# Token mixing placed between attention units, one PSUM pool for the whole program, and early conversion of four weight blocks

## The chip, the core and the metric

The kernel runs as one program on one NeuronCore of a Trainium2 chip. The metric is the time of one execution on the device in microseconds (us), measured from outside; three runs of the kernel before took 513.26, 514.47 and 515.23 us, median 514.47. Engines are named as in the profile: PE (TensorE matmuls; PEld is its weight load), DVE (VectorE), ACT (ScalarE), POOL (GpSimd) and SP (SyncE, which here issues the DMAs).

## What is computed

Two batches of 768 tokens pass through attention with 8 heads of 64 columns (a band of `n_local` = 96 keys behind each query, and `n_global` = 8 global keys, with a bias linear in distance), then through two mixing blocks. The calls chain as attention, `_moe_ref`, `_moe2_ref`; cut to what matters here:

```python
scores = scale * np.matmul(q, k.transpose(0, 1, 3, 2)) + bias      # kept in the band only
a = np.exp(scores - max);  a = a / (sum(a) + 1e-9);  x = a @ v      # x: (2, 768, 512)

xt = x.transpose(0, 2, 1)                       # _moe_ref: token mixing, then channel mixing
h  = np.maximum(xt @ w_tok1, 0.0) @ w_tok2      # 768 -> 256 -> 768 over tokens
u  = x + h.transpose(0, 2, 1)
x  = u + np.maximum(u @ w_ch1, 0.0) @ w_ch2     # 512 -> 1536 -> 512 over channels

theta = x @ w_theta                             # _moe2_ref
y = w_tok_r @ (x*cos(theta)) + w_tok_i @ (x*sin(theta))
out = (x + y) + np.maximum((x + y) @ w_ch, 0.0)
```

The weights arrive as 64-bit floats.

## The kernel before

Matrices of the mixing blocks are kept as two fp32r parts, a high and a low one, and each product is three matmuls (`mm3`: high by high, high by low, low by high).

**Jobs.** Each piece of a weight, 512 or 384 double words per partition, is loaded as raw words and converted on the chip by a "job" of four phases: `job_scale` (two ACT passes, lines 120 and 121), `job_join` (two DVE passes, lines 126 and 129, and one on POOL, line 130), `job_high` (ACT, line 138), `job_low` (DVE, line 141). One call of `tick` moves every running job by a phase, may start the next, and asks SP for further loads (two ahead, three raw buffers).

**Attention** (`attention_band`) goes over 24 units: batch, pair of heads, and two query blocks of 128; three units make up a pair of heads. In step u the code emits the scores of unit u (PE, line 383), per block and head the maximum with the bias (DVE, line 395) and the exponential (ACT, line 405); then, one by one in turn, the transposes of unit u-1 (PE, line 426, copied from PSUM by ACT, line 433) and the products with the values of unit u-2 (PE, line 350); then the division by the sum (`finish_rows`, DVE, lines 334 to 343), the split of x into its two parts (`x_split`, POOL, lines 323 and 326) and the tick. A job is started in the first unit of each pair of heads from the second pair on, seven in all: the weights of token mixing. The order on every engine is the order of this code. Scores use 4 PSUM banks, transposes 2, values 2.

**Mixing** (`moe`, after the attention, with new PSUM pools: 6 banks `acc`, 2 banks `wps`). The first product of token mixing (`token_mix`, "mm1": 18 matmuls for each of 2 batches and 2 blocks of 128 hidden tokens) runs for batch 0, block 0 in the last two steps of the attention, and for the other three blocks after it. `token_mix2` then runs the second product ("mm2") in 12 rows of 6 matmuls; DVE adds each row to x (line 803), and three rows later PE transposes it (line 621), ACT takes its high part (line 588) and DVE its low part (line 594). Every second row has a tick. `channel_mix` follows (`up`: matmuls "gp"; `down`: matmuls "h"), with the ticks for 24 channel jobs and for the weights of the last block, and then `PhaseB`.

**The start.** Whether the band form may be used depends on `n_global` and `n_local`: every engine loads these into registers (line 670), computes the condition and branches (line 678). The bias of the band (`band_bias`) is built from the same numbers, which DMA brings into the tile `nvi`: some dozen short DVE operations, and then one scaled copy for each of the 8 heads on POOL (line 273).

Of the kernel before, what the change touches and what calls it, by code (L numbers as in the profile page):

```python
# [24 lines left out]
P = 128  # L25
# [9 lines left out]
NG = 32  # L35
# [11 lines left out]
WARM = 12  # L47
# [13 lines left out]
def r(ap):  # L61
    return ap.bitcast(F32R)


class Build:
# [84 lines left out]
    def prefetch(self):  # L150
        while self.jobs and len(self.loaded) < self.AHEAD:
            job = self.jobs.pop(0)
            self.job_load(job)
            self.loaded.append(job)
# [7 lines left out]
    def tick(self, start=True):  # L162

        phases = (self.job_scale, self.job_join, self.job_high, self.job_low)
        for job in self.running:
            job["phase"] += 1
            phases[job["phase"]](job)
# [3 lines left out]
        self.prefetch()  # L171
        if start and self.loaded and self.loaded[0]["gate"] <= self.gate:
            job = self.loaded.pop(0)
            job["phase"] = 0
            phases[0](job)
            self.running.append(job)

# [10 lines left out]
    def constants(self, pool):  # L188
        nc = self.nc
        self.ident = pool.tile([P, P], F32, name="ident")  # L190
        make_identity(nc, self.ident)

        nvi = pool.tile([P, 4], I32, name="nvi")
        nc.sync.dma_start(out=nvi, in_=self.dram["nv"].broadcast_to([P, 4]))
        nvf = pool.tile([P, 4], F32, name="nvf")
        nc.vector.tensor_copy(out=nvf, in_=nvi)
# [11 lines left out]
        self.halfpi = pool.tile([P, 1], F32, name="halfpi")  # L208
        nc.vector.memset(self.halfpi, math.pi / 2)
        one = pool.tile([P, 1], F32, name="one")  # L210
        nc.scalar.activation(out=one, in_=self.halfpi, func=AF.Exp)

    def iota(self, pool, n, base, step, mult, name):
# [4 lines left out]
        return tf  # L218

    def band_bias(self, pool):  # L220
# [6 lines left out]
        ng, nl = self.nval[:, 0:1], self.nval[:, 1:2]  # L227
# [3 lines left out]
        with self.tc.tile_pool(name="bb", bufs=1) as tp:  # L231

            def ramp(n, base, mult, name):

                ti = tp.tile([P, n], I32, name=name + "_i")
                nc.gpsimd.iota(ti, pattern=[[1, n]], base=base, channel_multiplier=mult)
                tf = tp.tile([P, n], F32, name=name)
                nc.scalar.copy(out=tf, in_=ti)
                return tf

            def near(out, t, dist, tag):
# [7 lines left out]
            d_own = ramp(P, 0, -1, "own")  # L249
            d_prev = ramp(PREV, -PREV, -1, "prev")  # L250
            gcol = ramp(NG, 0, 0, "gcol")
            past = tp.tile([P, P], F32, name="past")
            nc.gpsimd.affine_select(
                out=past, in_=d_own, pattern=[[-1, P]], compare_op=ALU.is_ge, fill=-BIG,
                base=0, channel_multiplier=1,
            )
            nnl = tp.tile([P, 1], F32, name="nnl")
            nc.vector.tensor_scalar(out=nnl, in0=nl, scalar1=-1.0, scalar2=None, op0=ALU.mult)
            g = tp.tile([P, NG], F32, name="far_g")
            nc.vector.tensor_scalar(  # L260
                out=g, in0=gcol, scalar1=ng, scalar2=-BIG, op0=ALU.is_ge, op1=ALU.mult
            )
            nc.vector.tensor_scalar(out=seen, in0=g, scalar1=nl, scalar2=None, op0=ALU.subtract)
            near(own, past, d_own, "own")
            nc.vector.tensor_tensor(
                out=base0[:, 0:NG], in0=own[:, 0:NG], in1=seen, op=ALU.max
            )
            nc.vector.tensor_copy(out=base0[:, NG:P], in_=own[:, NG:P])
            near(before, d_prev, d_prev, "prev")
        self.base = []  # L270
        for h in range(H):
            t = pool.tile([P, 3 * P], F32, name="base%d" % h)
            nc.gpsimd.tensor_scalar(
                out=t, in0=base, scalar1=slope(h) / SCALE, scalar2=None, op0=ALU.mult
            )
# [4 lines left out]
    def warm_up(self, pool, n):  # L280

        ps = pool.tile([P, 512], F32, name="warm%d" % self.uid(), tag="o")
# [12 lines left out]

    def load_v(self, pool, t, b, hp, band=True):


        nc = self.nc
        n = "_%d_%d" % (b, hp)  # L300

# [840 lines left out]
```

## Time and profile before

| | |
|---|---|
| median of three runs | 514.47 us |
| profiled execution: time from outside / span of the trace | 513.04 / 511.0 us |
| start to the first maximum of unit 0 | 0 to 8.43 us |
| attention, 24 units | to 95.1 us |
| rest of mm1, three blocks | 96.44 to 109.07 us |
| mm2 and transposes, 12 rows | 109.07 to 132.10 us |
| channel mixing and PhaseB, to the last matmul | 132.10 to 507.9 us |

A row of a list of instructions begins with its start and its length in us, then engine, line of the kernel, operation, output<-input. The length of a matmul includes the filling and emptying of the array, so that neighbours overlap: the pace of PE is read from one start to the next. What stands in brackets is the idle time before the instruction and what ended it.

### The profile page before, as it was taken

What the parts mean: (1) busy time and instruction counts of PE and PEld (TensorE: products, weight loads), DVE (VectorE), ACT (ScalarE), POOL (GpSimd) and SP (SyncE); (2) the same over time, 40 slices, a digit from 0 to 9 for tenths busy, and PEclk for the clock granted to TensorE, in tenths of its full rate; (3) what the DMA queues carried; (4) which work ended last, traced back from release to release, by engine and by line L of the source; (5) the groups of instructions that cost most, each with busy time, mean ns of one, the idle gap of its engine ahead of it and who ended that gap; (6) DMA issues with size and microseconds to landing.
All of it is one profiled execution on the core that took longest, in us unless ns stands there. A gap on an engine that the chain in (4) does not pass through costs nothing.

```text
span 511.0 us, 7727 instructions
## 1 busy us (share of the span) xinstructions
PE 498.8 (98%) x2910; PEld 421.6 (83%) x2910; DVE 303.0 (59%) x669; ACT 238.9 (47%) x463; POOL 166.6 (33%) x175
## 2 busy tenths in 40 slices
PE   7999999999899999999999999999999999999997
PEld 3887888787788888888888888888888888888886
DVE  4677776269985754114655465387888885452352
ACT  4888878347665551102454453444555434132010
POOL 6654454133333331000333141234555543222000
PEclk9999999999999999999999999999999999999999
DMA  7867645144444440001433111321220000000012
GB/s 230 271 204 196 176 128 182 47 124 137 141 145 145 129 130 0 1 0 42 123 125 124 42 41 50 115 84 48 86 73 1 1 1 1 21 22 21 22 62 104
DMA packets 29724, 45.93 MB, mean 90 GB/s; under 512 B 1904, under 2 KB 20592, under 8 KB 29680
## 3 DMA queue, kind: packets, MB, share of 16 engines
q1 hardware_dynamic: 29680, 45.36, 29.1%
q8 instruction: 25, 0.41, 0.3%
q14 instruction: 19, 0.16, 0.1%
HBM read 42.21 MB, written 3.15 MB: 89 GB/s over the span
## 4 chain that ended last, share of the span: by engine, by line
PE 88%; DVE 7%; ACT 2%; DMA 1%; issue 1%; DVEq 0%; ACTq 0%
PE gp L77 20%; PE y L77 20%; PE h L77 19%; PE th L77 7%; PE v L77 7%; PE o L350 6%; PE t L426 4%; PE s L383 3%; PE mm L77 3%; ACT e L405 1%; DVE x L803 1%; DVE cvs L126 1%; DVE xl L594 1%; DVE cvt L129 1%; DVE wc L141 1%
## 5 line engine op out<-in xcount | busy, mean ns | idle before, releaser
L130 POOL TENSOR_TENSOR cvt<-cvt,cvs 128x512 int32<-128x512 int32 (+1 forms) x57 | 75.8, 1330 | 211.5 <-DVE cvt L129 197.0
L77 PE MATMUL h<-wc,g 128*128 128x512 f32 x432 | 102.2, 390 | 0.0
L77 PE MATMUL gp<-xh,wc 128*128 128x512 f32 (+1 forms) x384 | 99.0, 339 | 1.6 <-DVE xl L594 1.6
L77 PEld LDWEIGHTS h<-wc,g 128*128 128x128 f32 x432 | 79.6, 188 | 15.5
L590 DVE SCALAR_TENSOR_TENSOR g<-gp,g 128x512 fp32r<-128x512 f32 (+1 forms) x48 | 26.7, 557 | 91.2 <-ACT g L588 91.2
L77 PEld LDWEIGHTS gp<-xh,wc 128*128 128x128 f32 x384 | 67.1, 188 | 11.1 <-DVE xl L594 1.8
L77 PE MATMUL gp<-xl,wc 128*128 128x512 f32 (+1 forms) x192 | 64.9, 338 | 0.0
L588 ACT ACTIVATE g<-gp 128x512 fp32r<-128x512 f32 (+1 forms) x48 | 23.5, 489 | 78.8 <-PE gp L77 78.8
L77 PE MATMUL y<-wri,z 128*128 128x256 f32 (+1 forms) x288 | 52.9, 338 | 0.0
L77 PE MATMUL y<-wri,s 128*128 128x256 f32 (+1 forms) x288 | 52.8, 338 | 0.0
L426 PE MATMUL t<-ident,e 128*128 128x128 f32 x176 | 48.0, 285 | 3.5 <-ACT at L433 3.5
L77 PEld LDWEIGHTS y<-wri,s 128*128 128x128 f32 x288 | 44.9, 188 | 6.8
L77 PEld LDWEIGHTS y<-wri,z 128*128 128x128 f32 x288 | 44.8, 188 | 6.7
L405 ACT ACTIVATE e<-e,mn 128x256 f32<-128x256 f32 (+1 forms) x96 | 39.3, 481 | 17.5 <-DVE mn L395 17.5
L126 DVE SCALAR_TENSOR_TENSOR cvs<-cvt,cvs 128x512 int32<-128x512 int32 (+1 forms) x57 | 43.9, 770 | 0.0
L426 PEld LDWEIGHTS t<-ident,e 128*128 128x128 f32 x176 | 31.7, 185 | 11.7 <-ACT at L433 11.3
L77 PEld LDWEIGHTS gp<-xl,wc 128*128 128x128 f32 x192 | 36.1, 188 | 5.2
L120 ACT ACTIVATE cvt<-raw 128x512 f32<-128x512 f32 (+1 forms) x57 | 37.6, 659 | 2.2 <-issue 2.2
L121 ACT ACTIVATE cvs<-raw 128x512 int32<-128x512 uint16 (+1 forms) x57 | 37.6, 660 | 0.0
L395 DVE CUSTOM_DVE_ANT_0 e<-s,base 128x256 f32<-128x256 f32 (+1 forms) x96 | 32.8, 395 | 5.3 <-PE s L383 2.7
L932 ACT ACTIVATE w<-w 128x512 f32<-128x512 f32 x12 | 7.6, 632 | 57.3 <-DVE w L929 57.3
L350 PE MATMUL o<-v,at 128*128 128x65 f32 x192 | 32.3, 252 | 0.0
(140 smaller groups left out, 799.1 us busy)
## 6 DMA issues: line engine op xcount, KB each, us to landing
raw<-w_ch SPq DMA_DIRECT2D x28, 512.0 KB, 3.5
raw<-w_tok SPq DMA_DIRECT2D x21, 512.0 KB, 3.5
k<-k SPq DMA_DIRECT2D x8, 480.0 KB, 4.0
q<-q SPq DMA_DIRECT2D x8, 384.0 KB, 3.2
v<-v SPq DMA_DIRECT2D x8, 384.0 KB, 4.2
out<-o SPq DMA_DIRECT2D x11, 256.0 KB, 2.0
raw<-w_theta SPq DMA_DIRECT2D x4, 512.0 KB, 3.5
a<-v SPq DMA_DIRECT2D x8, 240.0 KB, 4.7
```

Source lines behind the costliest of these rows:

```text
L77: self.nc.tensor.matmul(out, lhsT=a, rhs=b, start=first and i == 0, stop=last and i == n - 1)
L120: nc.scalar.activation(out=f(t), in_=f(top), func=AF.Copy, scale=2.0**-111)
L121: nc.scalar.activation(out=s, in_=nxt, func=AF.Copy, scale=2.0**-13)
L126: nc.vector.scalar_tensor_tensor(out=s, in0=t, scalar=-(1 << 31), in1=s, op0=ALU.bitwise_and, op1=ALU.bitwise_or)
L130: nc.gpsimd.tensor_tensor(out=t, in0=t, in1=s, op=ALU.add)
L350: self.nc.tensor.matmul(po[:, j * OW : j * OW + D + 1], lhsT=at, rhs=v[:, j * (D + 1) : (j + 1) * (D + 1)], start=first, stop=last,)
L383: nc.tensor.matmul(ps[j][:, ii, c0:], lhsT=t["q"][pj, i * P : (i + 1) * P], rhs=kf[pj, i * KW - P + c0 : i * KW + P], start=True, stop=True,)
L395: nc.vector.tensor_tensor_reduce(out=e, in0=ps[j][:, ii, c0:], in1=self.base[2 * hp + j][min(i, 1)], op0=ALU.add, op1=ALU.min, scale=-SCAL ...
L405: nc.scalar.activation(out=e, in_=e, func=AF.Exp, bias=mn[:, ii, j : j + 1], scale=-1.0,)
L426: nc.tensor.transpose(pt[:, ii, c, :], e[j][:, ii, c * P : (c + 1) * P], self.ident)
L588: nc.scalar.activation(out=hi, in_=ps, func=AF.Relu if relu else AF.Copy)
L590: nc.vector.scalar_tensor_tensor(out=lo, in0=ps, scalar=0.0, in1=f(hi), op0=ALU.max, op1=ALU.subtract)
```

## The change

- All PSUM tiles come from one pool for the whole program, with tags s (4 banks), o (1), m (1) and t (2); what was `acc` goes around s, s, s, s, o, m.
- mm1 of batch 0 stands in units 14 to 19 of the attention (two parts of 3 matmuls behind each unit), its mm2 rows in steps 20 to 25 and the first four of its transposes in steps 22 to 25; mm1 of batch 1 and the last two transposes stand at the end of the attention. `token_mix2` has the 6 rows of batch 1 alone.
- From unit 12 on the values of all units use the one bank o (before that o and m in turn).
- Eleven jobs are started in the attention, at units given by a table: the seven of token mixing and four channel pieces, which get buffers of their own.
- Within a unit the DVE passes of jobs stand behind the maxima, and in the units that start a job behind one of the copies as well; two of the four exponentials stand behind the first copy of the transposes, and the ACT passes of jobs ahead of the second. In units that start a job, up to unit 19, DVE makes the first copy.
- The start: register loads and branch stand ahead of the bias; the bias takes its numbers without the 64-bit arithmetic, two of its steps are on POOL; ACT makes the scaled copies of heads 0 and 1; q and k of the first pair of heads come in two pieces each, and v after the branch; 10 warm-up matmuls instead of 12.

```diff
+class Banks:
+    BUFS = dict(s=4, o=1, m=1, t=2)
+        self.round = itertools.cycle("ssssom")
+    def tile(self, shape, dtype, name, tag):
+        if tag == "acc":
+            tag = next(self.round)
+        return self.pool.tile(shape, dtype, name=name, tag=tag, bufs=self.BUFS[tag])
...
+    def split_tick(self, start):
+        on_act = [job for job in self.running if job["phase"] % 2]
+        on_dve = [job for job in self.running if not job["phase"] % 2]
+        def act():
+            self.advance(on_act)
+            self.begin(start)
+        return functools.partial(self.advance, on_dve), act
...
         for h in range(H):
             t = pool.tile([P, 3 * P], F32, name="base%d" % h)
-            nc.gpsimd.tensor_scalar(
-                out=t, in0=base, scalar1=slope(h) / SCALE, scalar2=None, op0=ALU.mult
-            )
+            if h < 2:
+                nc.scalar.activation(out=t, in_=base, func=AF.Copy, scale=slope(h) / SCALE)
+            else:
+                nc.gpsimd.tensor_scalar(
...
+                        if j == 1:
+                            between()
+                        if j == 0 and dve:
+                            nc.vector.tensor_copy(out=af, in_=pf)
+                        else:
+                            nc.scalar.copy(out=af, in_=pf)
...
-                po = ps_o.tile([P, 2, 2 * OW], F32, name="o" + n, tag="o")
+                tag = "m" if u < half and u % 2 else "o"
+                po = ps_.tile([P, 2, 2 * OW], F32, name="o" + n, tag=tag)
...
+            for n in range(2 * NS):
+                tb, s = divmod(n, NS)
+                fill[half + 2 + n // 2].append(mix1(0, tb, s, "m"))
+            for s in range(NS):
+                fill[N - 4 + s].append(mix2(s))
+            for s in range(4):
+                fill[N - 2 + s].append(columns(s))
+            for tb in range(NT):
+                for s in range(NS - 2):
+                    fill[N + 1].append(mix1(1, tb, s, "s"))
...
+                start = u in self.STARTS
+                on_dve, on_act = self.split_tick(start)
...
-                    scores(u)
+                    exps = scores(u)
-                else:
-                    self.token_mix(ps_s, h1, 0, 0, tag="s", part=u - N)
+                if not start:
+                    on_dve()
+                for step in exps[:2]:
+                    step()
+                def between(late=exps[2:]):
+                    for step in late:
+                        step()
+                    if start:
+                        on_dve()
+                    on_act()
...
-                if oi:
-                    self.tick(start=u < N and ip == 0)
+                for step in fill.pop(u, ()):
+                    step()
...
+            for tb in range(NT):
+                for s in range(NS - 2, NS):
+                    mix1(1, tb, s, "s")()
+            for s in range(4, NS):
+                columns(s)()
...
+    EARLY = 4
+    STARTS = (5, 8, 11, 13, 14, 16, 17, 18, 20, 21, 22)
...
-        for b, tb in ((0, 1), (1, 0), (1, 1)):
-            self.tick()
-            self.token_mix(acc, h1, b, tb)
-        self.tick()
-        pend = self.token_mix2(acc, wps, h1)
+        pend = self.token_mix2(h1)
```

Three places where the order of instructions differs. First, DVE at the start of the program, before; `nv` are the two numbers as registers, `base` the bias, `s_0` the scores and `mn` the maxima of unit 0.

```order
L265 TENSOR_TENSOR base<-base 128x32
L247 TENSOR_TENSOR base<-farprev,prev 128x96
L670 TENSOR_LOAD nv_ptr
L670 TENSOR_LOAD nv
L678 ISA
L678 REGISTER_ALU
L678 ISA
L678 REGISTER_ALU x2
L678 COMPARE_AND_BRANCH
L395 ISA e_0_337,mn_336<-s_0_339,base_181 128x128
```

The same engine after the change, from its first memset on.

```order
L851 MEMSET zero 128x256
L225 MEMSET halfpi 128x1
L856 TENSOR_LOAD nv_ptr
L856 TENSOR_LOAD nv
L861 ISA
L861 REGISTER_ALU
L861 ISA
L861 REGISTER_ALU x2
L861 COMPARE_AND_BRANCH
L287 CAST nvf<-nvi 128x4
L294 TENSOR_SCALAR nnl<-nvf 128x1
L299 TENSOR_SCALAR farown<-ramp_130,nnl 128x128
```

The loads and the branch have moved from between the bias and the first maximum to ahead of the bias.

Second, DVE in a unit in which a job is joined, before (unit 8; `cvs` and `cvt` are the job's tiles, `o` the products with the values).

```order
L343 TENSOR_TENSOR x_83<-o_668,rc_689 128x2x128
L126 SCALAR_TENSOR_TENSOR cvs_648<-cvt_647,cvs_648 128x512
L129 TENSOR_SCALAR cvt_647<-cvt_647 128x512
L395 ISA e_8_712,mn_711<-s_8_714,base_189 128x256
L395 ISA mn_711 128x1
```

And after (unit 6).

```order
L447 ISA e_6_595,mn_593<-s_6_597,base_310 128x256
L447 ISA mn_593 128x1
L142 SCALAR_TENSOR_TENSOR cvs_585<-cvt_584,cvs_585 128x512
L145 TENSOR_SCALAR cvt_584<-cvt_584 128x512
L387 TENSOR_SCALAR rc_636<-o_611 128x4
L391 RECIPROCAL rc_636<-rc_636 128x4
```

The job's two passes stood ahead of the unit's four maxima and now stand behind them, ahead of `finish_rows`.

Third, PE between the values of a unit and the scores of unit 23, before.

```order
L350 MATMUL o_1442<-v_2_1172,at_20_1403 128x65
L350 MATMUL o_1442<-a_2_1175,at_20_1403 128x65
L350 MATMUL o_1442<-v_2_1172,at_20_1403 128x65
L383 MATMUL s_23_1475<-k_3_1169,q_3_1168 128x256
L383 MATMUL s_23_1476<-k_3_1169,q_3_1168 128x256
```

And after (`mm_0_2` is row 2 of mm2 of batch 0, `ut_0` the transposes of its row 0).

```order
L403 MATMUL o_1528<-a_2_1195,at_20_1478 128x65
L403 MATMUL o_1528<-v_2_1193,at_20_1478 128x65
L93 MATMUL mm_0_2_1565<-h_0_79,w_84 128x512 x6
L760 MATMUL ut_0_1573<-ident,x_64 128x128 x4
L434 MATMUL s_23_1583<-k_3_1201,q_3_1200 128x256
L434 MATMUL s_23_1584<-k_3_1201,q_3_1200 128x256
```

Ten matmuls of token mixing now stand between two units; steps 14 to 25 each have 6 to 10 of them, and step 25, behind its 10, 24 more of mm1 of batch 1.

## Rows read from the trace of the kernel before

**Rows 1.** By stage: us, busy us (instructions) of PE, PEld, DVE, ACT, POOL; clock; DMA

```profile
14.50:86.80 72.30, 69.16 (x632) 59.04 (x631) 53.05 (x249) 60.92 (x144) 36.76 (x64) 1.00 0.67 196
109.10:132.10 23.00, 21.23 (x109) 16.80 (x107) 21.99 (x39) 15.88 (x28) 7.56 (x6) 1.00 0.46 141
132.10:507.90 375.80, 375.76 (x1992) 321.57 (x1992) 213.70 (x323) 145.18 (x255) 106.03 (x79) 1.00 0.20 62
```

**Rows 2.** What PE waited for, 14.5 to 86.8 us: total us, times, longest

```profile
PE t L426 <- ACT at L433: 3.1, 6, 0.7
```

**Rows 3.** Chain of waits inside one unit, 63 to 68 us: start, length, what

```profile
63.61 0.42 DVE x L343
64.03 0.48 DVE cvs L126
...
64.97 0.33 DVE e L395
...
67.11 0.48 ACT at L433
...
67.64 0.33 PE t L426
```

**Rows 4.** PE instructions at the end of the attention

```profile
94.87 0.39 PE L350 MATMUL o<-v,at 128*128 128x65 f32 x2
96.44 0.48 PE L77 MATMUL mm<-xh,w 128*128 128x512 f32 x1 [1.19 <-DVE x L343]
```

**Rows 5.** Branch of line 678 on PE: shortest/median/longest ns, first and last start

```profile
L678 PEldq COMPARE_BRANCH  x2: 97/1724/3352, 5.3 to 92.9; - x2
```

**Rows 6.** PE instructions of the mm2 stage

```profile
114.66 0.60 PE L621 MATMUL ut<-ident,x 128*128 128x128 f32 x4
115.02 1.64 PE L77 MATMUL mm<-h,w 128*128 128x512 f32 x6
116.49 0.60 PE L621 MATMUL ut<-ident,x 128*128 128x128 f32 x4
132.10 0.50 PE L77 MATMUL gp<-xh,wc 128*128 128x512 f32 x1 [1.57 <-DVE xl L594]
```

**Rows 7.** Chain of waits in the mm2 stage: start, length, what

```profile
119.89 0.60 DVE x L803
120.49 0.60 DVE xl L594
121.08 0.60 DVE wc L141
121.68 0.61 DVE cvs L126
122.32 0.43 DVE cvt L129
```

**Rows 8.** Chain of waits at the start: start, length, what

```profile
0.74 3.00 DMA nvi<-nv
...
5.91 0.11 DVE base L265
...
8.43 0.13 DVE e L395
...
8.85 3.09 ACT e L405 x8
```

**Rows 9.** Register loads of line 670: shortest/median/longest ns, first and last start

```profile
L670 ACTq TENSOR_LOAD <-nv_ptr x1: 3167/3167/3167, 2.0 to 2.0; - x1
L670 ACTq TENSOR_LOAD <-nv x1: 969/969/969, 5.2 to 5.2; - x1
```

**Rows 10.** Costliest groups: busy us, mean ns of one, idle before

```profile
L120 ACT ACTIVATE cvt<-raw 128x512 f32<-128x512 f32 (+1 forms) x57 | 37.6, 659 | 2.2 <-issue 2.2
```

**Rows 11.** POOL's split of x, 14 to 96 us: shortest/median/longest ns

```profile
L323 POOL TENSOR_SCALAR xh<-x x23: 403/638/774, 15.9 to 92.3; 128x256 fp32r<-128x256 f32 x23
L326 POOL TENSOR_TENSOR xl<-x,xh x23: 727/732/779, 16.4 to 93.1; 128x256 fp32r<-128x256 f32 x23
```

More of the change, by code (lines that the diff above doesn't have):

```diff
@@ L1 @@
+import collections
 import functools
@@ L148, in start_jobs, with prefetch @@
         self.added = self.done = 0
-    def prefetch(self):
-        while self.jobs and len(self.loaded) < self.AHEAD:
+    def prefetch(self, ahead=AHEAD):
+        while self.jobs and len(self.loaded) < ahead:
             job = self.jobs.pop(0)
@@ L162, in tick, with advance @@
     def tick(self, start=True):
+        self.advance(list(self.running))
+        self.prefetch()
+        self.begin(start)
+    def advance(self, jobs):
         phases = (self.job_scale, self.job_join, self.job_high, self.job_low)
-        for job in self.running:
+        for job in jobs:
             job["phase"] += 1
@@ L170, in tick, with begin @@
             self.done += 1
-        self.prefetch()
+    def begin(self, start):
         if start and self.loaded and self.loaded[0]["gate"] <= self.gate:
@@ L247, in near @@
                 nc.vector.tensor_tensor(out=out, in0=far, in1=t, op=ALU.add)
[L249 to L255, printed above, removed]
-            )
[L257 to L263, printed above, removed]
             near(own, past, d_own, "own")
+            nc.scalar.copy(out=base0[:, NG:P], in_=own[:, NG:P])
+            near(before, d_prev, d_prev, "prev")
             nc.vector.tensor_tensor(
@@ L608, in token_mix, with token_row, turn_row, turn_rows @@
                 )
-                for s in ss
             ],
-            first=part != 1,
-            last=part != 0,
-        )
-        if part != 0:
-            self.evac_split(h1[b][:, 0, tb], h1[b][:, 1, tb], self.mm1, relu=True)
-    def turn_rows(self, ps, tag, src, hi, lo, name):
-        pt = ps.tile([P, NE, P], F32, name=name, tag=tag)
+            first=s == 0,
+            last=s == NS - 1,
+        )
+        if s == NS - 1:
+            self.evac_split(h1[b][:, 0, tb], h1[b][:, 1, tb], mm1, relu=True)
+    def token_row(self, tag, h1, b, s):
+        ps = self.ps.tile([P, E], F32, name="mm2_%d_%d" % (b, s), tag=tag)
+        cs = slice(s * P, (s + 1) * P)
+        self.mm3(
+            ps,
+            [
+                (
+                    (r(self.w2h[:, t, cs]), r(self.w2l[:, t, cs])),
+                    (h1[b][:, 0, t], h1[b][:, 1, t]),
+                )
+                for t in range(NT)
+            ],
+        )
+        x = self.x[b][:, s, :]
+        self.nc.vector.tensor_tensor(out=x, in0=ps, in1=x, op=ALU.add)
+    def turn_row(self, tag, b, s):
+        cs = slice(s * P, (s + 1) * P)
+        uth, utl = self.ut[b]
+        self.turn_rows(
+            tag, self.x[b][:, s, :], r(uth[:, :, cs]), r(utl[:, :, cs]), "ut_%d_%d" % (b, s)
+        )
+    def turn_rows(self, tag, src, hi, lo, name):
+        pt = self.ps.tile([P, NE, P], F32, name=name, tag=tag)
         for d in range(NE):
@@ L632, in token_jobs @@
             )
[L633 to L635 removed]
+        for h in range(2):
+            hs = slice(h * S // 2, (h + 1) * S // 2)
+            for t in range(NT):
                 self.add_job(
@@ L654, in run @@
                 self.xl.append(self.xs.tile([P, NS, E], F32, name="xl%d" % b, tag="xs"))
+            shape = lambda t: t.rearrange("p n e -> p (n e)").rearrange("p (d s) -> p d s", d=NE)
+            self.ut = [(shape(self.xh[b]), shape(self.xl[b])) for b in range(B)]
+            self.mm1 = {}
+            self.ps = Banks(es.enter_context(tc.tile_pool(name="ps", bufs=1, space=PSUM)))
             a8s = es.enter_context(ExitStack())
```

333 lines of the change are left out of this document (190 added, 143 removed).

## The prediction, written before the changed kernel was run

> **What bounds the kernel now.** I read the busy times by stage first, then what PE waited for in each stage, then the chain of waits at the places where PE stood still, and last the list of instructions there.
>
> The stages show one engine behind the whole program. From 132.1 us to the last matmul PE is busy 375.76 of 375.80 us [rows 1], and none of that work is removed or added, so nothing can be won there. What can be won lies ahead of 132.1 us, in the holes between matmuls and in the start. A busy share does not show such holes well, since the records of neighbouring matmuls overlap; I take them from starts and waits:
>
> - Attention, from the first dense unit on (21 units in 72.3 us): PE waits 3.1 us in 6 places, always a transpose for ACT's copy [rows 1, 2]. Without that a unit takes (72.3 - 3.1)/21 = 3.30 us. So PE is nearly full here as well: the reader should see that the matmuls put between these units cannot be free, they can only fill 3 us of holes.
> - The end of the attention: PE stands still for 1.2 us ahead of the matmul that starts at 96.44 [rows 4].
> - The mm2 stage: a row costs PE 116.49 - 114.66 = 1.83 us where nothing is in the way, 0.36 for four transposes and 1.47 for six matmuls [rows 6]. Twelve rows and the nine transpose groups of this stage come to 12 x 1.47 + 9 x 0.36 = 20.9 us; it took 23.0. Its bound is DVE, busy 21.99 of 23.0 [rows 1]: two rows and one job step are two additions to x, two low parts and three job passes, 2 x 0.60 + 2 x 0.60 + 0.60 + 0.61 + 0.43 = 4.04 us [rows 7], against 3.66 on PE. Most of what is lost is the 1.57 us for which the first "gp" waits [rows 6].
> - The start: the bias is done at 6.0 and the first maximum comes at 8.43 us; the 2.4 us between are DVE's register loads and branch [rows 8].
>
> Holes and start together are 3.1 + 1.2 + 2.1 + 2.4 = 8.8 us; with what the filling of the pipeline may give, that is the ceiling.
>
> **The change part by part.**
>
> *The start.* DVE's loads move ahead of the bias, beside the 3.0 us in which it waits for `nvi` anyway. Loads issued early are slow, though: ACT's began at 2.0 and ended at 6.2 [rows 9]. If DVE's begin about 1.2 and take as long as ACT's, they end at 5.3; the branch's register steps are an estimated 0.8 of the 2.4 us above; then come seven short DVE steps, where thirteen took 2.3 us [rows 8], so 1.3; then a scaled copy on ACT, 0.5 by the exponentials' 3.09/8 = 0.39 on fewer columns. First maximum at 7.9; ACT's own loads, branch and copies lead to much the same time. Best case: loads and branch are hidden behind `nvi`, first maximum at 3.74 + 1.3 + 0.5 = 5.6, gain 2.8; worst: no gain. I take -0.6, nearest to ACT's row. The smaller first pieces of q and k, two warm-up matmuls less and v after the branch lie beside this path; were v late, the values of unit 0 would wait, which eats at most this gain. Then the first copy of the transposes follows six exponentials instead of eight, 0.8 us less, but ACT's sum of work is the same: -0.4.
>
> *Order within a unit.* In the unit shown the job's passes hold DVE from 64.03 to 64.97, four maxima, the exponentials and the copy follow, and PE's transpose starts when the copy is through [rows 3]. Taking 0.94 us of passes from ahead of the maxima removes this, and the first copy no longer stands behind all four exponentials. What is late next is the second copy, now behind the job's ACT passes; it is needed only by the second half of the values in the next step, some 2 us later. Of 3.1 us I take -2.6; bounds -3.1 and +2 (second copy late by 0.3 us in half of the units before the filling starts).
>
> *Token mixing between the units.* 36 matmuls of mm1, 36 of mm2 and four transpose groups enter steps 14 to 25: 72 x 0.245 + 4 x 0.36 = 19.1 us at the pace of [rows 6]. The stages behind lose the same amount, so PE's sum is unchanged; each change of shape might cost a few hundredths, two per step: +0.4 (bounds 0 and 1.2). Does DVE follow? It gets 6 additions to x, 4 low parts and 2 low parts of mm1, 12 x 0.60 = 7.2, four more jobs of 1.64 = 6.6 [rows 7] and eight copies of 0.48 [rows 3] = 3.8: 53.05 + 17.6 = 70.7 busy in about 72.3 + 19.1 - 3.1 = 88 us. ACT gets four jobs of three passes and six further copies, at most 18 x 0.66 = 11.9 [rows 10], and gives eight copies away: at most 72.8 in 88. On average both fit. The tightest step is 23: maxima 4 x 0.35, a low part and a join 1.64, the division, whose last step takes 0.42 [rows 3], about 0.8, addition and low part 1.2: 5.0 us against 3.30 + 1.47 + 0.36 = 5.1 on PE. I allow +0.4 for waits in steps 20 to 25; bounds 0 and 4. The single value bank is covered: between the last value matmul of one unit and the first of the next stand 1.5 us of token mixing and the scores, an estimated 1 us of the unit's 3.30, while the division ends about 1 us after the former. The four further loads are issued two jobs ahead, some 10 us in these longer units, beside DMA engines that are 0.67 busy [rows 1].
>
> *The end of the attention.* The profile names DVE's x as what ended the 1.2 us hole, but PE's jump over the other branch of the program started at 92.9 and took 3.35 us, to 96.25, 0.2 us before that matmul [rows 4, 5]. I hold the jump for the cause. After the change up to 12 x 0.245 + 2 x 0.36 = 3.7 us of work stand behind the last wait and ahead of the jump: -0.9 (bounds 0 and -1.2). If x is the cause, 24 matmuls of mm1 of batch 1 cover it too.
>
> *The mm2 stage.* Six rows of batch 1 with three ticks remain, of twelve rows with six, and no job is yet at its last pass: 6 additions, 3 low parts and two joins, 5.4 + 2.1 = 7.5 us of DVE against 6 x 1.47 + 3 x 0.36 = 9.9 on PE. DVE no longer binds: -2.1 (bounds 0 and -2.1). The first row waits for the low part of mm1's last block, two passes of 0.6 behind its matmuls; two transpose groups and three matmuls, 1.4 us, cover that. In channel mixing the conversion runs closer to its use: four pieces are done early, but only 3 ticks are over at the first `up` instead of 10; each job is then complete three ticks, or one and a half blocks, ahead of its use, so nothing waits.
>
> Sum: -0.6 - 0.4 - 2.6 + 0.4 + 0.4 - 0.9 - 2.1 = -5.8 us. The profiled execution took 513.04 (2.0 of it outside the span), 1.4 below the median of the three runs. 513.04 - 5.8 = 507.2; on the scale of the median 508.6.
>
> A case against more DVE work beside POOL: POOL's high part of x takes 0.40 us at its shortest and up to 0.77, its low part stays at 0.73 [rows 11]; in this trace POOL is stretched, and nothing waits for it but matmuls a unit later. The Trainium skill says, in "SBUF — State Buffer", section "SBUF: two separate sides", that a DVE instruction with two SBUF inputs and a GpSimd instruction share a port pair as an exclusive lock: whichever starts first holds it, and the other blocks. The stretched rows agree with that for POOL; no run here shows DVE blocked. By that rule DVE is the loser where POOL starts first, which is rival 3 below.
>
> **The rivals.**
>
> 1. *Everything goes.* Start fully behind `nvi` (-2.8), pipeline -0.8, holes -3.1, -1.2, -2.1, nothing new: -10.0, time 504.5. For it: the loads by average. Against: slow early register loads [rows 9].
> 2. *Only the seams.* The exponentials behind the copy make ACT wait for transposes in the units before 14, so the 3.1 us stay, and the start gives nothing: -0.9 - 2.1 + 0.8 = -2.2, time 512.3. For it: ACT is busy 84% there [rows 1] and cannot run ahead.
> 3. *DVE blocked by POOL.* If each of the eight two-input passes of the four added jobs stands 0.73 us behind POOL's low part [rows 11], DVE is 5.8 us longer in steps 20 to 25, which have little to spare: -5.8 + 5.4 = -0.4, time 514.1. Against: the division now comes last in a unit, so POOL works while DVE does additions and maxima.
> 4. *Slower.* The single value bank in steps 14 to 25: if DVE's queue brings the division later than 2.5 us after the last value matmul, PE waits in every such step, with the scores of the next unit behind it. At 1.0 us in 12 steps: 12 - 6.2 = +5.8, time 520.3. It makes the kernel slower from about 0.75 us per step on. Against: the sums of the step above.
>
> **How the numbers follow.** Chances: forecast 0.60, everything 0.13, seams 0.15, DVE blocked 0.04, slower 0.08. Half a per cent, 2.6 us, is what a measurement tells from no change, so faster means below 511.9. The forecast lies there but for 0.02, rival 1 does, rival 2 one time in three: 0.58 + 0.13 + 0.05 = 0.76. Same: 0.02 + 0.10 + 0.03 of rival 3 = 0.15. Slower: 0.08 + 0.01 = 0.09. The range, 504.0 to 513.0, takes in rivals 1 and 2 and leaves out 3 and 4 and the tails of the rest; the forecast's own is 506 to 511.
>
> **What would show it.** Right: PE's waits for ACT's copies below 1 us in all ahead of step 14; the first maximum between 7.3 and 8.2; steps 14 to 19 near 3.3 + 1.5 = 4.8 us, 22 and 23 near 5.1; no hole above 0.5 us at the end of the attention or before the first "gp"; the stretch from the first "gp" to the end as long as before. Wrong: value matmuls waiting for DVE's x (rival 4), job passes on DVE stretched (rival 3), transposes waiting for copies in units 3 to 13 (rival 2), or a change behind the first "gp", which nothing here accounts for.

## The result and the profile after

The changed kernel takes 506.9 us (median of 4 runs, 506.54 to 507.1) against 514.49 us (4 runs): ratio 0.9854, 95% interval 0.9834 to 0.9874. Its profiled run took 506.85 us from outside, 505.1 us of span; before it was 513.04 and 511.0. The first view is again the one of busy times by stage (us, busy us of PE, PEld, DVE, ACT and POOL, granted clock, share of the DMA engines, GB/s): start, units 3 to 13, steps 14 to 22, the end of the attention with mm1 of batch 1, the mm2 rows of batch 1, and all behind the first "gp".

```profile
0.00:13.95 13.95, 12.32 (x66) 6.74 (x67) 6.49 (x36) 8.95 (x23) 9.54 (x22) 1.00 0.58 179
13.95:50.06 36.11, 36.11 (x332) 31.11 (x332) 28.85 (x131) 30.33 (x72) 17.21 (x31) 1.00 0.79 240
50.06:92.90 42.84, 42.84 (x329) 34.73 (x328) 35.00 (x131) 32.87 (x76) 19.53 (x32) 1.00 0.56 178
92.90:116.14 23.24, 22.56 (x143) 19.02 (x142) 12.57 (x32) 9.37 (x20) 6.14 (x9) 1.00 0.15 47
116.14:126.17 10.03, 9.95 (x48) 7.97 (x48) 6.89 (x13) 3.98 (x8) 1.10 (x1) 1.00 0.28 79
126.17:501.96 375.79, 375.75 (x1992) 321.56 (x1992) 219.06 (x331) 150.21 (x265) 109.92 (x82) 1.00 0.21 67
```

The last stage is as long as it was, 375.79 against 375.80 [rows 1]: the whole difference between the two traces, 132.10 - 126.17 = 5.9 us, lies ahead of the first "gp". PE now has no gap from 13.95 to 92.90, and DVE no longer binds the mm2 rows (busy 6.89 of 10.03 us; it was 21.99 of 23.0).

PE's waits, 14 to 45 us and then 45 to 100 us, answer to [rows 2] (total us, times, longest). The six waits of transposes for ACT's copies are gone; one of 0.34 us is left in step 24, behind the stretch of [rows 2]:

```profile
PE s L434 <- DMA k<-k: 0.4, 1, 0.4
...
PE t L481 <- ACT at L493: 0.3, 1, 0.3
```

The length of a step is read from one start of the scores to the next: 3.37 us without token mixing (46.69 to 50.06), 4.84 with two parts of mm1 behind the unit (step 19, 73.49 to 78.33). The steps with a mm2 row alone, 20 and 21, take 4.56 and 4.74 us, and step 22, with a row and a transpose group, 5.27 (87.63 to 92.90).

```profile
46.69 1.14 PE L434 MATMUL s<-k,q 64*128 64x256 f32 x8
50.06 1.13 PE L434 MATMUL s<-k,q 64*128 64x256 f32 x8
73.49 1.14 PE L434 MATMUL s<-k,q 64*128 64x256 f32 x8
78.33 1.13 PE L434 MATMUL s<-k,q 64*128 64x256 f32 x8
```

The end of the attention (PE's list, and PE's jump, line 861; shortest, median, longest ns), for [rows 4, 5]. The jump still takes 3.63 us, but it starts while mm1 of batch 1 is in PE's queue. It ends at 112.5 + 3.63 = 116.1, and that is where the remaining hole of 0.34 us ends:

```profile
116.14 5.87 PE L93 MATMUL mm<-h,w 128*128 128x512 f32 x24 [0.34 <-ACT xh L704]
```

```profile
L861 PEldq COMPARE_BRANCH  x2: 98/1862/3627, 4.2 to 112.5; - x2
```

The last mm2 rows and the first "gp", for [rows 6]: a row takes 1.83 us (123.67 to 125.50), PE's own pace, and "gp" waits for nothing, where it had waited 1.57 us.

```profile
123.67 0.60 PE L760 MATMUL ut<-ident,x 128*128 128x128 f32 x4
125.50 0.60 PE L760 MATMUL ut<-ident,x 128*128 128x128 f32 x4
126.17 0.50 PE L93 MATMUL gp<-xh,wc 128*128 128x512 f32 x1
```

The start, for [rows 8]: the first maximum (DVE's list) comes at 7.29 instead of 8.43 us. But the scores of unit 3, the fourth, start at 13.95 where it was 14.45, so only 0.5 of these 1.14 us is left. The chain of waits says that k of the second pair of heads, issued at 8.10, is late. Six more traces with this start (experiments 4 to 8 and 12) agree: the first maximum comes at 6.49 to 7.01 us, unit 3 waits 0.34 to 1.24 us for this k, and its scores start at 13.46 to 14.33. What the start gives thus differs from trace to trace by some 0.9 us, and 0.5 is a value near the middle.

```profile
7.29 0.29 DVE L447 CUSTOM_DVE_ANT_0 e<-s,base 128x128 f32<-128x128 f32 x1 [1.44 <-PE s L434]
```

```profile
8.10 5.71 DMA k<-k
...
13.95 0.34 PE s L434
```

Two things are open with this. The medians differ by 7.6 us and the traces by 5.9 to 6.2; and each term of the sum was only read off, not tried.

### The profile page after: what moved, and what is told of

Same layout as the page of the kernel before. It is cut to its first block, busy times and chain, and to the rows that moved or that the text cites. A ratio compares the mean times of both kernels' runs of the same rounds, so it can differ in the third digit from the quotient of the medians.

```text
span 505.1 us, 7724 instructions
## 1 busy us (share of the span) xinstructions
PE 499.5 (99%) x2908; PEld 421.1 (83%) x2908; DVE 309.3 (61%) x671; ACT 235.7 (47%) x458; POOL 163.4 (32%) x175
## 4 chain that ended last, share of the span: by engine, by line
PE 95%; SPq 1%; DMA 1%; ACT 1%; DVE 1%; issue 0%; ACTq 0%
PE gp L93 20%; PE y L93 20%; PE h L93 19%; PE th L93 7%; PE v L93 7%; PE mm L93 6%; PE o L403 6%; PE t L481 4%; PE s L434 4%; DMA k<-k 1%; PE ut L760 1%; SPq L856 0%; DVE xl L710 0%; ACT xh L704 0%; PE xt_1p L760 0%
## 5 line engine op out<-in xcount | busy, mean ns | idle before, releaser
L403 PEld LDWEIGHTS o<-v,at 128*128 128x128 f32 x192 | 29.8, 196 | 0.0
```

The lines of the kernel that those rows point to most:

```text
L403: self.nc.tensor.matmul(po[:, j * OW : j * OW + D + 1], lhsT=at, rhs=v[:, j * (D + 1) : (j + 1) * (D + 1)], start=first, stop=last,)
```

## The experiments

Times are medians; "level" is the mean granted clock of a run.

**1. Another trace of the kernel before.**

> The kernel before, unchanged, for a second trace. The two traces so far differ by 5.9 us (511.0 against 505.1 us of span), the medians of the runs by 7.6 us. If the first trace of before was a quick one by chance, a second one lies 1 to 2 us higher, and the place where it differs from the first names what varies; if the difference lies outside the span, the second span is 511 as well.

Measured 513.12 us, span 511.2, clock 1.0: as the first trace. The 18 runs of before beside it show what varies: 9 have a mean clock of 0.997 and take 514.4 to 515.3 us, the others 0.999 or 1.0 and 512.8 to 513.7. Over the three comparisons of this study it is 19 of 46 (median 514.85) against 27 (513.28). So the median of before depends on how many of its runs have the lower clock, and the profiled run had the higher; experiment 2 caught the other kind.

**2. The order on DVE alone, in the kernel before.** `split_tick` here returns the DVE passes as `finish`, called behind the scores of the next unit:

```diff
-                    self.tick(start=u < N and ip == 0)
+                    finish = self.split_tick(start=u < N and ip == 0)
```

> The kernel before with one part of the change alone: DVE's job passes (join and low part) stand behind the next unit's maxima instead of ahead of them. Everything else, ACT's order and the token mixing too, is as before. If the passes ahead of the maxima are what PE waited for in the attention (3.1 us in 6 waits of transposes for ACT's copies), those waits fall below 1 us and the time by 2 to 2.6 us, ratio about 0.995 to 0.996. Rival (only the seams): ACT's full queue sets these waits, they stay near 3 us and the ratio is 1.000.

511.8 us, ratio 0.9945 (0.9924 to 0.9965). PE's waits from 14.5 to 83.8 us, in the form of [rows 2]:

```profile
PE o L376 <- DMA a<-v: 0.3, 1, 0.3
PE t L452 <- ACT at L459: 0.2, 1, 0.2
```

The waits fall from 3.1 to 0.5 us, and those for ACT's copies to 0.2: the order of DVE's passes is the whole of this term, and rival 2 falls. Between runs of the same level the gain is 513.28 - 510.0 = 3.3 us (3 runs) and 514.85 - 512.24 = 2.6 us (4 runs at 0.997). The profile is of such a run, and shows where the clock goes (stages of 2 us, columns as above; the last but two is the granted clock):

```profile
92.00:94.00 2.00, 0.68 (x6) 0.57 (x6) 1.30 (x5) 0.53 (x1) 0.46 (x2) 1.00 0.00 0
94.00:96.00 2.00, 2.00 (x7) 1.58 (x7) 0.00 (x0) 0.69 (x2) 0.68 (x1) 0.65 0.18 41
96.00:98.00 2.00, 2.00 (x6) 1.54 (x5) 0.00 (x0) 0.00 (x0) 0.00 (x0) 0.50 0.73 244
98.00:100.00 2.00, 2.00 (x10) 1.65 (x9) 0.00 (x0) 0.12 (x1) 0.00 (x0) 1.00 0.01 2
```

PE is busy 0.68 of 2.00 us around the hole at the end of the attention (1.32 us), and behind it the granted clock is 0.50, the 1.2 GHz level, until about 98 us. The 54 matmuls of mm1 behind the hole take 14.18 us here (93.82 to 108.00) and took 12.63 in the first trace of before (96.44 to 109.07), where the clock stayed at 1.00. These 1.6 us are the distance of before's two levels, 514.85 - 513.28.

**3. The hole of before filled with matmuls of zeros.**

```diff
+                if u == N + 1:
+                    self.warm_up(ps_o, 8)
```

> The kernel before with eight matmuls of zeros (128x512, nothing reads them) behind the last value matmuls, ahead of PE's jump. Of the runs of before about half show a mean clock of 0.997 and take 1.6 us longer; in the trace of the kernel with the order alone, such a run, the granted clock is 0.50 from 95 to 98 us, behind the hole of 1.3 us at the end of the attention. If that hole is what brings the slow clock, filling it ends the two levels: every run at a mean clock of 1.0, spread below 0.8 us, at 513.2 + 8 x 0.24 - (hole 1.2 less a rest of 0.3) = 514.2 us. Rival: the clock falls for another reason, and half of the runs stay 1.6 us longer than the other half.

514.28 us, and all 12 runs lie within 514.16 to 514.52 at a clock of 0.999 or 1.0, where of 46 runs of before 19 did not. At that place:

```profile
95.15 1.89 PE L284 MATMUL warm<-zero 128*128 128x512 bf16 x8
97.64 0.47 PE L77 MATMUL mm<-xh,w 128*128 128x512 f32 x1 [0.61 <-ACT cvs L121]
```

```profile
L680 PEldq COMPARE_BRANCH  x2: 97/1760/3422, 5.2 to 94.1; - x2
```

So the hole is what brought the low clock in these runs. It costs before its 1.2 us and, in 4 of 10 runs, some 1.6 more. The other hole of before, 1.57 us ahead of the first "gp", is as long in this kernel, and the granted clock is 1.00 behind it. The last row gives the jump once more: 94.1 + 3.42 = 97.5, and the matmul behind it starts at 97.64, whatever releaser the list names.

**4. mm1 of batch 1 behind the jump**, and with it the last two transpose groups:

```diff
-            for tb in range(NT):
-                for s in range(NS - 2):
-                    fill[N + 1].append(mix1(1, tb, s, "s"))
...
+        for s0, s1 in ((0, NS - 2), (NS - 2, NS)):
+            for tb in range(NT):
+                for s in range(s0, s1):
+                    self.token_part("s", h1, 1, tb, s)
```

> The changed kernel with mm1 of batch 1 and the last two transpose groups behind PE's jump over the other branch of the program instead of ahead of it. PE then reaches the jump with 12 matmuls and 2 transpose groups less behind its last wait. If the jump is the cause of the hole at the end of the attention, a hole of 0.9 to 1.3 us stands ahead of the first matmul of mm1 of batch 1 and the time is 507.8 to 508.2 us. If DVE's x was the cause, the hole follows x: most of mm1 of batch 1 does not need the last x, so there is no hole and the time stays at 506.9.

507.22 us (506.65 to 508.25), the profiled run 0.8 above that of the changed kernel. The median is below the forecast and the times overlap with those of the changed kernel, so the times alone settle nothing; the trace does. The hole is there:

```profile
107.72 0.51 PE L93 MATMUL mm<-xh,w 128*128 128x512 f32 x1 [0.78 <-POOL xl L379]
```

```profile
L853 PEldq COMPARE_BRANCH  x2: 98/1870/3642, 4.2 to 104.0; - x2
```

104.0 + 3.64 = 107.6: again the matmul follows the jump. The list names POOL's xl of the last unit, which this matmul (rows 0 of x) does not read. The jump is the cause. The hole is 0.78 instead of 0.9 to 1.3, since a mm2 row and a transpose group still stand behind PE's last wait: PE works on for 2.9 us after the start of the jump, where it was 2.3 in before.

**5. DVE's passes ahead of the maxima again, in the changed kernel.**

```diff
+                    on_dve()
                     exps = scores(u)
...
-                if not start:
+                else:
                     on_dve()
...
-                    if start:
-                        on_dve()
```

> The changed kernel with DVE's job passes ahead of the maxima again in every unit; the exponentials and ACT's passes keep the new order. If the order on DVE is what freed the 2.8 us, waits of transposes for ACT's copies come back in the units ahead of step 14, fewer jobs being there (three starts instead of four), so 1.5 to 2.5 us in all, and 508.4 to 509.4 us. In the steps with token mixing behind them PE has 1.5 us of other work, so there they need not come back. Rival: the split exponentials or the work between the units did it, and nothing comes back: 506.9 us.

514.58 us (513.87 to 517.3; the 7 of 12 runs at a clock of 0.999 or 1.0 have a median of 514.12), the profiled run 7.2 us above the changed kernel: three to five times the forecast. Ahead of step 14 the steps are 2.6 us longer (38.75 instead of 36.11), about as forecast. The rest comes where none was expected, 1.8 us in steps 14 to 22 and 2.4 from step 23 to the mm2 rows of batch 1. The chain of waits in step 21 shows how:

```profile
86.53 0.89 ACT e L577 x2
87.42 0.52 ACT wc L154
87.94 0.57 ACT cvt L136
88.51 0.56 ACT cvs L137
...
89.09 0.70 DVE cvs L142
...
89.82 0.43 DVE cvt L145
90.24 0.20 DVE e L447
...
90.86 0.39 ACT e L573
91.24 0.17 ACT at L493
...
96.19 0.09 ACT at L493
```

ACT's job passes, now ahead of the second copy, feed DVE's join directly. DVE's join stands ahead of the maxima, the maxima feed the exponentials, and behind the first copy stand the next exponentials and job passes. It is a loop over two engines: one turn takes 4.95 us (91.24 to 96.19), more than PE's 4.5 to 4.8 in steps 14 to 21. In the kernel before, ACT's passes ran a whole step ahead of DVE's. So this is not the change's order undone but a worse one than before: it shows that ACT's new order needs DVE's passes behind the maxima.

**6. ACT's order as before.** All four exponentials ahead of the copies, job passes behind both:

```diff
-                for step in exps[:2]:
+                for step in exps:
...
-                def between(late=exps[2:]):
-                    for step in late:
-                        step()
+                def between():
...
-                    on_act()
...
+                on_act()
```

> The changed kernel with ACT's order within a unit as before: all four exponentials ahead of the copies, ACT's job passes behind both copies; DVE's order stays new. If DVE's order is the whole of the gain in the units, as the order alone in the kernel before suggests (waits from 3.1 to 0.2 us), nothing comes back: 506.9 us, steps as long as now. If ACT's split order carries a share, the first copy stands behind two more exponentials, 0.9 us, and transposes wait again, 0.3 us in some units: 507.5 to 509 us.

506.81 us (506.45 to 507.19), every step from 3 to 22 within 0.02 us of the changed kernel's. With DVE's passes behind the maxima, ACT's split order is worth nothing here.

**7. Token mixing of batch 0 behind the attention**, mm1, mm2 rows and transposes, which for this take the banks s, o and m:

```diff
-                fill[half + 2 + n // 2].append(mix1(0, tb, s, "m"))
...
+                tail.append(mix1(0, tb, s, "sm"[tb]))
```

> The changed kernel with all token mixing of batch 0 (mm1, the six mm2 rows, the four transpose groups) behind the last unit of the attention instead of between the units; the order within a unit, the eleven job starts and the start stay. PE's sum of work is the same. If the place between the units is what pays (it gives DVE and ACT the time for the four further jobs), the units from 12 on, again 3.3 us long, wait: four jobs of 1.64 us of DVE in 12 units, and the mm2 rows at the end wait for DVE's additions; +1 to +4 us, so 508 to 511 us. Rival: the order within a unit and the moved job starts alone did it, the place of the matmuls is indifferent: 506.9 us, with the units near 3.3 us and no hole at the end.

520.21 us (profiled run 518.22), ratio 1.0122 (1.0095 to 1.0149): well beyond the forecast, and slower than before. From step 15 to 22 the steps take up to 5.10 us instead of 3.3, 4.9 us in all, and the chain lies on DVE:

```profile
72.03 0.63 DVE w L157
72.67 0.61 DVE cvs L142
...
73.30 0.43 DVE cvt L145
...
74.05 0.43 DVE x L396
...
74.73 0.29 PE o L403
```

This is the prediction's slower rival: job passes bring the division late, and the value matmuls wait for their one bank (5 waits, 4.7 us, the longest 1.3). With holes in PE's stream the clock falls too, to 0.60 in one stretch of 4 us:

```profile
PE o L403 <- DVE x L396: 4.7, 5, 1.3
```

```profile
88.00:92.00 4.00, 2.93 (x18) 2.53 (x17) 2.55 (x6) 2.62 (x7) 2.82 (x3) 0.75 0.73 243
92.00:96.00 4.00, 2.98 (x23) 2.88 (x23) 1.36 (x4) 1.17 (x3) 1.28 (x2) 0.83 0.00 0
96.00:100.00 4.00, 4.00 (x15) 3.31 (x15) 0.77 (x3) 0.00 (x0) 1.36 (x3) 0.60 0.01 2
```

By these rows the clock costs at most (0.25 + 0.17 + 0.40) x 4 = 3.3 us, and no run of the six is above 0.993. The longer steps and the clock are 8.2 of the 11.4 us between the profiled runs; most of the rest is two more waits for the bank behind step 22, 1.02 us each, and a hole of 1.47 instead of 0.34 us behind PE's jump. What the token mixing between the units buys is thus, above all, DVE's time for the eleven jobs.

**8. One value bank for all units.**

```diff
-                tag = "m" if u < half and u % 2 else "o"
+                tag = "o"
```

> The changed kernel with the one value bank o for all units, those ahead of unit 12 too, where no token mixing stands between the units. This prices the bank that the prediction's slower rival spoke of. Between the last value matmul of a unit and the first of the next stand only the scores and a transpose there, 1.3 us on PE; the division takes DVE about 0.8 us once it starts. If DVE reaches it in time, nothing changes: 506.9 us. If the bank is held by DVE's queue, value matmuls wait 0.2 to 0.5 us in each of 10 steps: 509 to 512 us.

507.05 us (506.64 to 507.31); the steps 5 to 13 are longer by up to 0.09 us, 0.4 us in all. The bank alone costs next to nothing; it takes a late division as in experiment 7 to make it dear.

**9. The low part of the jobs on POOL in before's mm2 stage.**

```diff
+            self.nc.gpsimd.tensor_scalar(
+                out=x, in0=x, scalar1=2.0**-8, scalar2=None, op0=ALU.mult
+            )
+            self.nc.gpsimd.tensor_tensor(out=r(job["lo"]), in0=x, in1=job["hi"], op=ALU.subtract)
```

> The kernel before with the low part of the jobs on POOL instead of DVE in the six ticks of the mm2 stage, in two POOL passes (scale, subtract); nothing else moved. DVE's work for two rows and a tick falls from 4.04 to 3.43 us, below PE's 3.66. If DVE bounds the mm2 stage, it shrinks from 23.0 to about 21.2 us, and the time by 1.5 to 2 us (ratio 0.996 to 0.997). If POOL's passes hold DVE up as long as they take themselves (the prediction's third rival), DVE's additions and low parts are stretched and the stage stays at 23 us or grows.

518.46 us, ratio 1.0081 (1.0059 to 1.0103). Five of the six runs have a clock of 0.993 to 0.996; the one at 1.0 took 516.0 us. Neither theory holds: POOL's three passes of a tick (mean ns in the second column behind the bar) make 4.5 us, from 115.5 to 133.8 us they follow one another almost without a gap, and POOL itself becomes the bound, with 27.8 us for the stage.

```profile
L145 POOL TENSOR_SCALAR cvt<-cvt 128x512 f32<-128x512 f32 x5 | 9.4, 1885 | 0.0
L130 POOL TENSOR_TENSOR cvt<-cvt,cvs 128x512 int32<-128x512 int32 x6 | 8.2, 1368 | 6.3 <-DVE cvt L129 6.3
L148 POOL TENSOR_TENSOR wc<-cvt,wc 128x512 fp32r<-128x512 f32 x5 | 6.4, 1278 | 0.4
```

It doesn't tell whether DVE bound the stage before. What it shows is DVE beside a busy POOL (same stage, DVE's passes):

```profile
L812 DVE TENSOR_TENSOR x<-mm,x 128x512 f32<-128x512 f32 x12 | 8.0, 678 | 0.0
...
L129 DVE TENSOR_SCALAR cvt<-cvt 128x512 int32<-128x512 int32 x7 | 5.1, 732 | 0.2
L126 DVE SCALAR_TENSOR_TENSOR cvs<-cvt,cvs 128x512 int32<-128x512 int32 x6 | 4.9, 817 | 0.0
```

In the kernel before these are 681, 427 and 682 ns in that stage. The additions, which read PSUM, are as quick as ever; the job passes are stretched.

**10. v ahead of SP's branch.** The call behind the branch moves ahead of the register loads:

```diff
-            self.load_v(first, 0, 0)
...
                     self.tiles_v(p0, first, 0, 0)
+                    self.load_v(first, 0, 0)
```

> The changed kernel with the loads of v of the first pair of heads issued ahead of SP's register loads and branch instead of behind them. In the trace of the changed kernel SP issues nothing from 3.0 to 6.1 us, and the scores of unit 3 wait 0.44 us for k of the second pair, issued at 8.1 behind branch and v. If SP's queue at the branch is the cause, q and k go out 1.5 us earlier, the wait is gone and the scores of unit 3 start at 13.5 instead of 13.95: -0.4 us, 506.5. If the DMA engines are full anyway, k lands as late as before: 506.9. A loss would come from the register loads: with v's bytes under way they take longer, and the branch with the first maximum is late.

506.34 us (506.27 to 506.58; one value bank in the same comparison 506.64 to 507.31). The wait for k is gone and the scores of unit 3 start at 13.41, as forecast (13.46 to 14.33 in the seven traces with v behind the branch), but not for the reason given. SP's list:

```profile
8.72 0.35 SPq L335 DMA_DIRECT2D q<-q  x1
9.12 0.42 SPq L336 DMA_DIRECT2D k<-k  x1
```

SP's register loads took 2.29 + 0.50 us instead of 1.50 + 0.68, and k is issued 1.0 us later than before (9.12 against 8.10), not earlier. It lands 3.8 us after its issue instead of 5.7, since v's bytes are no longer ahead of it: the DMA engines, not SP's queue, held k.

**11. A shorter start.** As 10, with q and k of the second pair in two pieces each, and

```diff
-WARM_FILL = (4, 2)
+WARM_FILL = (2, 1)
...
+        for i0, i1 in ((0, 2), (2, NS)) if (b, hp) == (0, 1) else ((0, NS),):
```

> The changed kernel with v of the first pair ahead of the branch (as in the run before, 506.34 us), q and k of the second pair in two pieces each, and 3 instead of 6 matmuls of zeros behind the scores of units 0 and 1. In the trace with v ahead the maxima of unit 1 wait 0.70 us for its scores, which stand behind four matmuls of zeros. If PE's queue there bounds the filling of the pipeline, three such matmuls less, 3 x 0.25, let the scores of unit 3 start 0.4 to 0.75 us earlier, at 12.7 to 13.0: 505.6 to 506.0 us. If the exponentials bound it, nothing moves: 506.3. If PE, idle longer between the first scores, falls to the slow clock, it costs 1 us or more: above 507.3 us.

506.48 us (505.98 to 506.72): no better. What is late next is q of the first pair, whose second piece now shares the DMA engines with v and takes 5.54 us to land (4.2 in experiment 10, with the same loads beside it); the scores of unit 3 start at 13.52.

```profile
8.26 1.14 PE L437 MATMUL s<-k,q 64*128 64x256 f32 x8 [1.40 <-DMA q<-q]
```

**12. The changed kernel again.**

> The changed kernel, unchanged, beside the others of this comparison. If the two levels of before's time come from the hole at the end of the attention alone, every run of this kernel, which has no such hole, shows a mean clock of 0.999 or 1.0 and they lie within 0.8 us, near 506.9 us, while runs of before lie near 513.0 and 514.8. If the clock falls for another reason, some runs of this kernel lie 1.6 us higher too.

506.94 us; four runs 506.56 to 507.1 at 0.999 or 1.0, one of 509.03 at 0.996. With experiments 6, 8, 10 and 11 and the first four runs, the clock fell in 1 of 27 runs of kernels with at most 0.4 us of hole at the end of the attention, against 19 of 46 of before. Where it fell in the one isn't known; that run was not profiled. So the hole brings most of before's low clocks, but a low clock comes without it too. The ratio beside these runs of before (513.63 us) is 0.9875 (0.9854 to 0.9896).

## Why the prediction was right, and where not

The forecast was 508.6 us, -5.8; measured are 506.9 us, -5.9 between the traces. That the sums agree to 0.1 us is in part luck: the start gave 0.5 us less than forecast and the order 0.5 more, and the start alone differs by some 0.9 us between traces. By its own steps, read from the traces:

| step | predicted | measured |
|---|---|---|
| start and filling of the pipeline | -1.0 | -0.5 (scores of unit 3 at 13.95, were 14.45; -0.1 to -1.0 in seven traces) |
| order within a unit | -2.6 | -3.1 (all six waits; alone, experiment 2: 3.1 to 0.5) |
| changes of shape | +0.4 | about +0.3 in steps 14 to 22 (below) |
| waits in steps 20 to 25 | +0.4 | +0.3 (one wait, step 24) |
| end of the attention | -0.9 | -0.85 (1.19 to 0.34) |
| mm2 stage | -2.1 | -2.0 (23.0 - 20.9, less 10.03 - 9.9) |

- *Changes of shape*: steps 14 to 22 took 42.84 us. Nine units of 3.28 (the mean of units 3 to 13) make 29.5, 54 matmuls at the pace of an undisturbed stretch (36 in 8.39, experiment 5) 12.6, and a transpose group 0.4; 0.3 is left. The prediction counted these matmuls at 0.245 us each, the pace inside a mm2 row, which already holds its changes of shape; by that pace the term would be -0.3. No row of before had priced this term.
- *Right, and shown*: the order on DVE (experiments 2, 5, 6) and the jump (experiments 3 and 4; in the 11 traces with a hole there, the next matmul starts 0.0 to 0.2 us behind the jump's end). That mm2 was bound by DVE, the second largest term, is read from the trace alone: the chain of waits behind rows 7 runs over DVE alone from 118.69 us to the first "gp", and DVE's share fell from 21.99 of 23.0 to 6.89 of 10.03 while PE's gaps went. The run meant to try it (9) met another bound, so it is not shown by an experiment.
- *The start* was mis-sized. The early register loads took less than the row of ACT suggested (DVE 0.92 + 1.37 us from 0.8 on, where ACT's had taken 3.17 + 0.97 [rows 9]), so the first maximum came at 7.29, where 7.9 was forecast and 7.3 to 8.2 named as the sign of being right. Even there DVE waited 1.44 us for the scores, which took 1.57 us in this trace; in the six other traces of this start they took 0.93, and the maximum came at 6.49 to 7.01. But half of the gain or more was given back at k of the second pair. "Beside this path", as the prediction put it for v, was wrong: v's loads stand ahead of q and k of the second pair in SP's queue and on the DMA engines, and unit 3 waits for k. With v moved ahead (experiment 10) unit 3 starts 1.04 us earlier than in before, which is the gain that was forecast for the start as changed.
- *The step that failed* is the last: the sum of -5.8 was put on the scale of the median of before by adding 1.4 us. That 1.4 was not noise that both kernels share. Two of the three runs behind that median lie at 514.4 to 515.3 us, where the runs of before with the lower clock lie (their own clocks are not on record), and the low clock went with the hole in nearly all runs. 507.2, on the scale of the profiled run, was the better number; this is 1.4 of the 1.7 us between forecast and result.
- *Rival 4* did not come, by the sums of DVE's work; experiments 7 and 8 show how near it stood: the bank is free only as long as 1.5 us of matmuls per step give DVE its time. *Rival 3* came in part: the shift (cvt) of 384 columns took 565 ns in steps 14 to 25 where it was 443, the join (cvs) 647 where it was 547, 0.9 us over four jobs, and nothing waited for it. In experiment 9 such passes reach 1.40 us. The Trainium skill's rule ("SBUF — State Buffer", section "SBUF: two separate sides") is an exclusive lock between GpSimd and a DVE pass that has two SBUF inputs or runs in a two-port mode, held for the whole instruction. It fits the joins, which have two inputs: of the six in that stage five ran into a POOL pass begun before them, and each of the five ended 0.55 us behind that pass (POOL from 128.02 to 129.30, the join from 128.90 to 129.85). It also fits the shift of 1.40 us (one input), which ended 0.3 us behind POOL's pass. But four other shifts, of 0.72 us instead of 0.43, began and ended inside POOL passes of up to 1.95 us; if the rule covers them, a lock held for the whole instruction would not allow that. The measured price is a stretch, of 20% (joins) and 70% (shifts) in the mean.

## What to carry to other kernels

Put work that fills a queue for others (conversion, prefetch) behind the operations that the next step of the pipeline waits for, and keep a whole step between its stages on two engines; then ask whether the engine has the time at all, and give it that by placing matmuls from a stage that lies idle for it. A hole in PE's stream costs more than its length where the clock falls behind it, and shows as two levels in the times: compare runs of one level before putting a difference down to the change. Price a term on the scale on which it was read. When a list names a releaser that the instruction doesn't read, look at the jumps and queues of the engine itself.

## What the runs showed of the hardware

- PE's jump over the other branch took 3.31 to 3.69 us in all 14 traces, whatever stood around it; the first branch took 0.10 us, and the same jump on ACT, DVE, POOL and SP 0.04 to 0.06 us (the kernel of experiment 2). The Trainium skill ("Runtime: NRT & Kernel Launch", section "Instruction fetch mechanics") says that a taken branch to code outside the prefetched window waits for a fetch of it. PE's time fits that; no run here separates the fetch. PE works off what is in its queue meanwhile: 2.3 us of mostly short matmuls in before, 3.3 us of long ones and transposes after the change.
- With a hole of 1.2 to 1.3 us at the end of the attention the mean clock was 0.997 in some runs and 0.999 or 1.0 in others of the same kernel (19 of 46 against 27). In the kernel of experiment 2, with a hole of 1.32 us, the profiled run is one of 0.997 and shows the 1.2 GHz level for 3 to 4 us behind the hole. With 0.61 us left of the hole the clock fell in none of 12 runs, with 0.78 us (experiment 4) in none of 5. The length alone does not decide: behind the hole of 1.57 us ahead of the first "gp" [rows 6] the granted clock is 1.00 in all four traces that have it (two of before, experiments 2 and 3).
- The scores of unit 0 took 1.57 us in the trace of the changed kernel and 1.53 in that of experiment 10, and 0.93 in the other seven traces of its start (experiment 11's included). The granted clock is given as 1.00 there in all that were compared; what makes the difference is not shown.
